# The second layer of a mixture of experts: two of three fp16 products of a term joined into one of 160 columns

## The chip, the cores and the metric

One core of a Trainium2 chip. The metric is the device time of one execution of the whole kernel in microseconds (us). TensorE is PE (PEld are its weight loads), VectorE is DVE, ScalarE is ACT, GpSimd is POOL, and SyncE (SP) starts the large transfers.

## What is computed

Attention over 8 batches, 8 heads, 576 positions and 64 columns a head (half of the heads with a local mask, half with a strided one); its result, 4608 tokens of 512 columns, goes through a mixture of 8 experts. Each token goes to the expert with the largest logit, and each expert takes at most 80 tokens, those with the largest gate weight:

```python
for e in range(E):
    ...
    h = np.maximum(x[tok_idx] @ w1[e], 0.0)          # 80x512 times 512x1024
    out[tok_idx] = gate_w[tok_idx, None] * (h @ w2[e])   # 80x1024 times 1024x512
```

The change is in the second product, `h @ w2[e]`.

## The kernel before

The first 235 us are attention, the gates and the choice of tokens. Then come the experts, the last 75 us, which the change touches.

Numbers are kept at fp32 accuracy by splitting: a weight is written as an upper part (fp16) and the rest (fp16), and so is an input. A product then has three terms: upper weights times upper input, upper weights times the rest, the rest of the weights times the upper input. `mm3` (lines 1148 to 1151) issues them as three matmuls of 80 columns (the 80 slots of an expert), each with its own load of 128x128 weights, all into the same place in PSUM. The term of the two rests is left out.

The weights come from HBM in 64 chunks of 512 KB (`wload`, L270), through eight staging tiles (`ring`, `raw`, `kst`). `wsplit` makes a chunk's two parts: ACT writes the upper part (L278), DVE the rest (L288). The next load of a staging tile is issued on SP's queue when DVE has read the tile. `spl` holds the parts of eight half layers.

The work goes by halves (`halves`): the first layer of an expert is `up`, the second `down_mm`. Their order is up(0), up(1), down(0), up(2), down(1), ..., up(7), down(6), down(7). In each half `weave` mixes the half's matmuls with two or three splits (by `BSPL`), and in an `up` half also with `xprep` (PE transposes the next expert's gathered tokens, ACT and DVE split them into `xe`, POOL starts a gather, L1092) and with `finish` (below) of the expert before. All engines execute their instructions in the order in which this emits them.

- `up` (L1153): for each of two groups, 4 x 4 x 3 matmuls into `hp`; ACT applies the ReLU and writes the upper part of `he` (L1164), DVE the rest (L1165). `he` is laid out part by part: first the eight blocks of the upper part, then those of the rest.
- `down_mm` (L1168): 4 x 8 x 3 = 96 matmuls into one tile `yp` of 320 columns, in two PSUM buffers; then ACT copies it to `y32` (L1185). For the last expert the eight blocks of the inner dimension are the outer loop, since its weights arrive last, and a product with zeros (L1172) opens the tile.
- `finish` (L1188): PE transposes `y32` (L1192), ACT multiplies by the gates (L1194), POOL scatters the rows to the output (L1195). It stands in the `up` half that follows the expert's `down_mm`, a little before the middle of it; for expert 6 in the last half, and for expert 7 at the end.

Of the kernel before, what the change touches and what calls it, by code (L numbers as in the profile page):

```python
# [9 lines left out]
F32 = mybir.dt.float32  # L10
BF16 = mybir.dt.bfloat16
F16 = mybir.dt.float16
I32 = mybir.dt.int32
U32 = mybir.dt.uint32
AF = mybir.ActivationFunctionType
ALU = mybir.AluOpType
AX = mybir.AxisListType
PSUM = bass.MemoryType.PSUM
DRAM = bass.MemoryType.DRAM

P = 128
B, H, S, D = 8, 8, 576, 64
DM = H * D
E, F = 8, 1024
# [6 lines left out]
SLOTS = 80  # L31
# [144 lines left out]
def moe_attention(ctx: ExitStack, tc, q, k, v, wg, w1, w2, cap, out):  # L176
    nc = tc.nc
# [10 lines left out]
    identb = const.tile([P, P], BF16, name="identb")  # L188
# [64 lines left out]
    def spl_of(h):  # L253
        return spls[h] if h < NPRE else (spls[NPRE:] + spls[:NPRE])[(h - NPRE) % len(spls)]
# [600 lines left out]
    for i in range(n + 2):  # L855
# [38 lines left out]
        if i in (18, 30):  # L894
            x = Bank()
# [4 lines left out]
        if i == n + 1:  # L900
            do_logits(B - 1)
            x = Bank()
# [171 lines left out]
    for j0 in range(0, NCAND, 8):  # L1074
        nc.vector.tensor_tensor(oh[:, j0:j0 + 8], iosl.unsqueeze(1).broadcast_to([P, 8, SLOTS]),
                                slot[:, j0:j0 + 8].unsqueeze(2).broadcast_to([P, 8, SLOTS]), op=ALU.is_equal)
        for j in range(j0, j0 + 8):
            nc.tensor.matmul(tab.rearrange("s e a -> s (e a)"), oh[:, j], val[:, j].rearrange("p e a -> p (e a)"),
                             start=(j == 0), stop=(j == NCAND - 1))
# [48 lines left out]
    ectx = ExitStack()  # L1128
    fp = ectx.enter_context(tc.tile_pool(name="fp", bufs=2))
    psx = ectx.enter_context(tc.tile_pool(name="psx", bufs=1, space=PSUM))  # L1130
    psh = ectx.enter_context(tc.tile_pool(name="psh", bufs=3, space=PSUM))
    psy = ectx.enter_context(tc.tile_pool(name="psy", bufs=2, space=PSUM))

    xes, hes, ys_ = {}, {}, {}
    zb = fp.tile([P, 4 * SLOTS], BF16, name="zb", bufs=1)
# [12 lines left out]
    def mm3(o, w, i, x, c, first, last):  # L1148
        nc.tensor.matmul(o, w[:, 0, i:i + P], x[:, 0, c], start=first, stop=False)  # L1149
        nc.tensor.matmul(o, w[:, 0, i:i + P], x[:, 1, c], start=False, stop=False)  # L1150
        nc.tensor.matmul(o, w[:, 1, i:i + P], x[:, 0, c], start=False, stop=last)  # L1151

    def up(h, e):  # L1153
        w, xe = spl_of(h), xes[e]
        he = hes[e] = fp.tile([P, 2, 8, SLOTS], F16, name="he")
        for f4 in range(2):
            hp = psh.tile([P, 4, SLOTS], F32, name="hp")
            for ff in range(4):
                for c in range(4):
                    mm3(hp[:, ff], w, F * c + P * (4 * f4 + ff), xe, c, c == 0, c == 3)  # L1160
                if ff < 3:
                    yield
            sl = slice(4 * f4, 4 * f4 + 4)
            nc.scalar.activation(he[:, 0, sl], hp, AF.Relu)  # L1164
            nc.vector.scalar_tensor_tensor(he[:, 1, sl], hp, 0.0, he[:, 0, sl], op0=ALU.max, op1=ALU.subtract)  # L1165
            yield

    def down_mm(h, e):  # L1168
        w, he = spl_of(h), hes[e]
        yp = psy.tile([P, 4, SLOTS], F32, name="yp")  # L1170
        if e == E - 1:
            nc.tensor.matmul(yp.rearrange("p f s -> p (f s)"), identb, zb, start=True, stop=False)  # L1172
        for c in range(8 if e == E - 1 else 0):
            for f in range(4):
                mm3(yp[:, f], w, DM * c + P * f, he, c, False, c == 7 and f == 3)
            yield
        for f in range(4 if e < E - 1 else 0):
            for c in range(8):
                mm3(yp[:, f], w, DM * c + P * f, he, c, c == 0, c == 7)
                if c == 3:  # L1180
                    yield
            if f < 3:
                yield
        y32 = ys_[e] = fp.tile([P, 4, SLOTS], F32, name="y32")
        nc.scalar.copy(y32, yp)  # L1185
        yield

    def finish(e):  # L1188
        y32 = ys_[e]
        yt = psy.tile([SLOTS, 4, P], F32, name="yt")  # L1190
        for f in range(4):
            nc.tensor.transpose(yt[:, f], y32[:, f], ident)  # L1192
        ys = fp.tile([SLOTS, DM], F32, name="ys")
        nc.scalar.activation(ys, yt.rearrange("s f p -> s (f p)"), AF.Copy, scale=gt[:, e:e + 1])  # L1194
        nc.gpsimd.indirect_dma_start(out=out, out_offset=bass.IndirectOffsetOnAxis(ap=ids[:, e:e + 1], axis=0),  # L1195
                                     in_=ys, in_offset=None, bounds_check=NT - 1, oob_is_err=False)
# [11 lines left out]
    for h, (e, w) in enumerate(halves):  # L1208
        tasks = [((down_mm if w else up)(h, e), 8, 0, 1)]
        m = BSPL[h % len(BSPL)]  # L1210
        tasks.append((splits(m), m, *WIN["b"]))
        if w == 0 and e + 1 < E:
            tasks.append((once(xprep, e + 1), 1, *WIN["bx"]))
        if w == 0 and e > 1:
            tasks.append((once(finish, e - 2), 1, *WIN["bf"]))
        if h == 2 * E - 1:
            tasks.append((once(finish, e - 1), 1, *WIN["bf"]))
        weave(*tasks)
        flush()
    finish(E - 1)  # L1220
    ms.close()
    ectx.close()
# [5 lines left out]
    with tc.If(flag > 0):  # L1228
        with tc.tile_pool(name="gp", bufs=1) as gp, tc.tile_pool(name="gw", bufs=1) as gw, \
# [18 lines left out]
            with tc.For_i(0, NT, P) as i:  # L1248
# [3 lines left out]
                x = gw.tile([P, DM], F32, name="gx")  # L1252
# [25 lines left out]
                for e in range(E):  # L1278
# [5 lines left out]
                    for f4 in range(2):  # L1284
                        hp = gps.tile([P, 4, P], F32, name="gt")
# [5 lines left out]
                    yp = gps.tile([P, DM], F32, name="gt")  # L1291
# [82 lines left out]
```

## Time and profile before

| | |
|---|---|
| time, median of 3 runs | 319.17 us (318.51 to 320.11) |
| profiled execution | 317.6 us, its span 315.9 us |
| PE busy | 265.2 us (84%), 5399 matmuls |
| DVE, ACT, POOL busy | 242.4, 225.3, 135.2 us |
| DMA | 84.27 MB, mean 267 GB/s |
| expert stage | from 235.95 us; last matmul of expert 7 at 308.21 us |

Times of the trace are counted from the start of the span. "Busy" of PE is a modelled figure, since matmuls overlap: a matmul's record lasts 0.20 us, while the next one starts 0.036 us later. A wait is put down to what released it; "issue" means that the engine waited for nothing that the profile shows.

### The profile page before, as it was taken

What the parts mean: (1) busy time and instruction counts of PE and PEld (TensorE: products, weight loads), DVE (VectorE), ACT (ScalarE), POOL (GpSimd) and SP (SyncE); (2) the same over time, 40 slices, a digit from 0 to 9 for tenths busy, and PEclk for the clock granted to TensorE, in tenths of its full rate; (3) what the DMA queues carried; (4) which work ended last, traced back from release to release, by engine and by line L of the source; (5) the groups of instructions that cost most, each with busy time, mean ns of one, the idle gap of its engine ahead of it and who ended that gap; (6) DMA issues with size and microseconds to landing.
All of it is one profiled execution on the core that took longest, in us unless ns stands there. A gap on an engine that the chain in (4) does not pass through costs nothing. (4 is left out here: it accounts for less than half of the span.)

```text
span 315.9 us, 12765 instructions
## 1 busy us (share of the span) xinstructions
PE 265.2 (84%) x5399; PEld 235.3 (74%) x5399; DVE 242.4 (77%) x487; ACT 225.3 (71%) x438; POOL 135.2 (43%) x156
## 2 busy tenths in 40 slices
PE   7997987998898899895979987967259969988891
PEld 7986876887767788875867866657249969988890
DVE  7497698989988699886678999361847987997860
ACT  1757777898798798795776876658107978987761
POOL 8658376267284367286265277013072221110012
PEclk9999999999999999998998999999776999999996
DMA  7999999899998799995789999689999999899501
GB/s 246 217 267 377 252 226 323 260 298 264 334 273 250 202 286 285 317 237 205 199 239 247 215 239 345 210 257 283 270 264 336 338 384 377 288 407 389 193 25 48
DMA packets 49375, 84.27 MB, mean 267 GB/s; under 512 B 23201, under 2 KB 23201, under 8 KB 49314
## 3 DMA queue, kind: packets, MB, share of 16 engines
q1 hardware_dynamic: 48290, 80.79, 86.4%
q0 software_dynamic: 1024, 2.62, 2.6%
q8 instruction: 44, 0.72, 1.0%
q14 instruction: 17, 0.14, 0.2%
HBM read 63.21 MB, written 20.19 MB: 264 GB/s over the span
## 5 line engine op out<-in xcount | busy, mean ns | idle before, releaser
L553 POOL TENSOR_TENSOR pb<-pb,sm 128x288 f32<-128x288 f32 (+2 forms) x32 | 34.9, 1092 | 61.1 <-DVE sm L551 44.3
L1150 PEld LDWEIGHTS <-spl 128*128 128x128 f16 x512 | 52.1, 102 | 3.7 <-issue 3.6
L1149 PEld LDWEIGHTS <-spl 128*128 128x128 f16 x512 | 52.1, 102 | 3.0 <-issue 3.0
L1151 PEld LDWEIGHTS <-spl 128*128 128x128 f16 x512 | 52.1, 102 | 2.1 <-issue 2.1
L461 POOL TENSOR_SCALAR vlo<-vlo 32x1152 f32<-32x1152 f32 (+1 forms) x32 | 37.7, 1179 | 6.8 <-DMA ring<-moe_w 2.2
L774 DVE SCALAR_TENSOR_TENSOR spl<-ring,spl 128x1024 f16<-128x1024 f32 x20 | 28.3, 1424 | 9.4 <-ACT spl L278 9.4
L1149 PE MATMUL hp<-xe,spl 128*128 128x80 f16 x256 | 31.7, 208 | 3.4 <-issue 2.8
L1150 PE MATMUL hp<-xe,spl 128*128 128x80 f16 x256 | 31.6, 207 | 1.4 <-issue 1.1
L1151 PE MATMUL hp<-xe,spl 128*128 128x80 f16 x256 | 31.6, 208 | 0.0
L598 PE MATMUL bank<-ptl,vlo 128*64 128x64 f32 x576 | 22.5, 228 | 9.4 <-issue 9.3
L353 ACT COPY ktl<-bank 64x384 f32<-64x384 f32 (+1 forms) x49 | 26.4, 566 | 4.8 <-DMA xs<-ktl 3.1
L1149 PE MATMUL yp<-he,spl 128*128 128x80 f16 x256 | 28.8, 202 | 1.2 <-issue 1.2
L1150 PE MATMUL yp<-he,spl 128*128 128x80 f16 x256 | 28.8, 202 | 1.1 <-issue 1.1
L1151 PE MATMUL yp<-he,spl 128*128 128x80 f16 x256 | 28.8, 202 | 0.4 <-issue 0.3
L1195 POOL DMA_INDIRECT out<-ys,ids x8 | 7.6, 950 | 50.1 <-ACT ys L1194 50.1
L598 PEld LDWEIGHTS bank<-ptl,vlo 128*64 128x64 f32 x576 | 19.5, 139 | 12.7 <-issue 10.6
L288 DVE SCALAR_TENSOR_TENSOR spl<-raw,spl 128x1024 f16<-128x1024 f32 x21 | 25.2, 1220 | 4.2 <-ACT spl L278 3.7
L278 ACT ACTIVATE spl<-ring 128x1024 f16<-128x1024 f32 x23 | 23.8, 1057 | 4.5 <-DMA ring<-moe_w 4.5
L353 ACT COPY ptl<-bank 64x256 f32<-64x256 f32 (+2 forms) x46 | 21.3, 473 | 6.8 <-PE bank L581 3.4
L549 DVE TENSOR_REDUCE sm<-pb 128x16 f32<-128x288 f32 (+2 forms) x32 | 22.8, 711 | 3.7 <-ACT pb L546 3.7
L546 ACT ACTIVATE pb<-pb 128x288 f32<-128x288 f32 (+2 forms) x32 | 18.1, 565 | 9.9 <-DVE pb L539 9.7
L353 ACT COPY xt<-bank 128x288 f32<-128x288 f32 (+3 forms) x40 | 16.8, 441 | 11.0 <-PE bank L598 7.7
(209 smaller groups left out, 752.7 us busy)
## 6 DMA issues: line engine op xcount, KB each, us to landing
ring<-moe_w SPq DMA_DIRECT2D x32, 512.0 KB
raw<-moe_w SPq DMA_DIRECT2D x21, 512.0 KB
raw<-q SPq DMA_DIRECT2D x16, 576.0 KB
out<-kst SPq DMA_DIRECT2D x9, 1024.0 KB
raw<-k SPq DMA_DIRECT2D x15, 576.0 KB
kst<-moe_w SPq DMA_DIRECT2D x11, 512.0 KB
xs<-xn SPq DMA_DIRECT2D x12, 384.0 KB
vs<-v SPq DMA_DIRECT2D x8, 512.0 KB
```

Of the source, the lines that this page charges most:

```text
L278: nc.scalar.activation(hi, r, AF.Copy, scale=SC)
L288: nc.vector.scalar_tensor_tensor(lo, r, SC, hi, op0=ALU.mult, op1=ALU.subtract)
L353: nc.scalar.copy(o, i)
L461: add(4 * b + m + 0.6 + 0.4 * u, "P", 1.25 if m == 0 else 1.1, lambda e: nc.gpsimd.tensor_scalar(vlo[64 * u:64 * u + 32, t0:t1], vlo[64 * ...
L546: add(pj(j) + E_EXP, "A", 0.13 + 0.83e-3 * nt * nk, lambda e: nc.scalar.activation(pa, pa, AF.Exp), wr=PN)
L549: nc.vector.tensor_reduce(each(sm[:, 0:nt], g), pq, op=ALU.add, axis=AX.X)
L553: add(pj(j) + E_MUL, "P", 0.2 + 1.7e-3 * nt * nk, lambda e: nc.gpsimd.tensor_tensor(plain(pa, g), plain(pa, g), spread(sm[:, 0:nt], g), op ...
L598: nc.tensor.matmul(o[64 * h:64 * h + 64, :, k0:k0 + 32], vlo[:, 2 * (t0 + c0 + c) + p, h], ptl[:, c0 + c, :, 32 * gg:32 * gg + 32], start= ...
L774: add(pr + 0.2, "V", 1.14, lambda e: nc.vector.scalar_tensor_tensor(lo, r, SC, hi, op0=ALU.mult, op1=ALU.subtract), rd=nm + [("hi", i)], l ...
L1149: nc.tensor.matmul(o, w[:, 0, i:i + P], x[:, 0, c], start=first, stop=False)
L1150: nc.tensor.matmul(o, w[:, 0, i:i + P], x[:, 1, c], start=False, stop=False)
L1151: nc.tensor.matmul(o, w[:, 1, i:i + P], x[:, 0, c], start=False, stop=last)
```

## The change

`mm2` takes the place of `mm3` in the second layer. One matmul multiplies the upper part of the weights by both parts of the input, 160 columns, into two neighbouring sums of 80 columns; a second one multiplies the rest of the weights by the upper part of the input and adds to the first of the two sums. For that `he` is laid out block by block, the two parts of a block side by side. The accumulator has twice the columns (640) and so takes two PSUM banks, `yp0` and `yp1`, one buffer each in place of two of one bank; `yt` keeps its two. ACT copies each bank to `y2`, the first when half of the half is done, and POOL adds the two sums into `y32`; for the last expert DVE adds. The zero product of the last expert becomes two. The first layer keeps `mm3`.

```diff
--- before.py
+++ after.py
@@ -1129,7 +1129,7 @@
     fp = ectx.enter_context(tc.tile_pool(name="fp", bufs=2))
     psx = ectx.enter_context(tc.tile_pool(name="psx", bufs=1, space=PSUM))
     psh = ectx.enter_context(tc.tile_pool(name="psh", bufs=3, space=PSUM))
-    psy = ectx.enter_context(tc.tile_pool(name="psy", bufs=2, space=PSUM))
+    psy = ectx.enter_context(tc.tile_pool(name="psy", bufs=1, space=PSUM))
 
     xes, hes, ys_ = {}, {}, {}
     zb = fp.tile([P, 4 * SLOTS], BF16, name="zb", bufs=1)
@@ -1152,7 +1152,8 @@
 
     def up(h, e):
         w, xe = spl_of(h), xes[e]
-        he = hes[e] = fp.tile([P, 2, 8, SLOTS], F16, name="he")
+
+        he = hes[e] = fp.tile([P, 8, 2, SLOTS], F16, name="he")
         for f4 in range(2):
             hp = psh.tile([P, 4, SLOTS], F32, name="hp")
             for ff in range(4):
@@ -1161,33 +1162,49 @@
                 if ff < 3:
                     yield
             sl = slice(4 * f4, 4 * f4 + 4)
-            nc.scalar.activation(he[:, 0, sl], hp, AF.Relu)
-            nc.vector.scalar_tensor_tensor(he[:, 1, sl], hp, 0.0, he[:, 0, sl], op0=ALU.max, op1=ALU.subtract)
+            nc.scalar.activation(he[:, sl, 0], hp, AF.Relu)
+            nc.vector.scalar_tensor_tensor(he[:, sl, 1], hp, 0.0, he[:, sl, 0], op0=ALU.max, op1=ALU.subtract)
             yield
+
+    def mm2(o, w, i, x, first, last):
+
+        nc.tensor.matmul(o.rearrange("p a s -> p (a s)"), w[:, 0, i:i + P], x.rearrange("p a s -> p (a s)"), start=first,
+                         stop=False)
+        nc.tensor.matmul(o[:, 0], w[:, 1, i:i + P], x[:, 0], start=False, stop=last)
 
     def down_mm(h, e):
         w, he = spl_of(h), hes[e]
-        yp = psy.tile([P, 4, SLOTS], F32, name="yp")
+        yp = [psy.tile([P, 2, 2, SLOTS], F32, name=f"yp{i}") for i in range(2)]
+        y32 = ys_[e] = fp.tile([P, 4, SLOTS], F32, name="y32")
+
+        def sums(i):
+            y2 = fp.tile([P, 2, 2, SLOTS], F32, name=f"y2{i}")
+            nc.scalar.copy(y2, yp[i])
+            (nc.vector if e == E - 1 else nc.gpsimd).tensor_tensor(y32[:, 2 * i:2 * i + 2], y2[:, :, 0], y2[:, :, 1], op=ALU.add)
         if e == E - 1:
-            nc.tensor.matmul(yp.rearrange("p f s -> p (f s)"), identb, zb, start=True, stop=False)
-        for c in range(8 if e == E - 1 else 0):
+            for t in yp:
+                nc.tensor.matmul(t.rearrange("p f a s -> p (f a s)"), identb, zb, start=True, stop=False)
+            for c in range(8):
+                for f in range(4):
+                    mm2(yp[f // 2][:, f % 2], w, DM * c + P * f, he[:, c], False, c == 7 and f % 2 == 1)
+                yield
+            for i in range(2):
+                sums(i)
+        else:
             for f in range(4):
-                mm3(yp[:, f], w, DM * c + P * f, he, c, False, c == 7 and f == 3)
-            yield
-        for f in range(4 if e < E - 1 else 0):
-            for c in range(8):
-                mm3(yp[:, f], w, DM * c + P * f, he, c, c == 0, c == 7)
-                if c == 3:
+                for c in range(8):
+                    mm2(yp[f // 2][:, f % 2], w, DM * c + P * f, he[:, c], c == 0, c == 7)
+                    if c == 3:
+                        yield
+                if f % 2:
+                    sums(f // 2)
+                if f < 3:
                     yield
-            if f < 3:
-                yield
-        y32 = ys_[e] = fp.tile([P, 4, SLOTS], F32, name="y32")
-        nc.scalar.copy(y32, yp)
         yield
 
     def finish(e):
         y32 = ys_[e]
-        yt = psy.tile([SLOTS, 4, P], F32, name="yt")
+        yt = psy.tile([SLOTS, 4, P], F32, name="yt", bufs=2)
         for f in range(4):
             nc.tensor.transpose(yt[:, f], y32[:, f], ident)
         ys = fp.tile([SLOTS, DM], F32, name="ys")
```

## Rows read from the trace of the kernel before

**Rows 1.** Windows: us, busy (count) of PE, PEld, DVE, ACT, POOL, PEclk, DMA share.
```profile
254.36:260.56 6.20, 5.06 (x128) 4.92 (x129) 4.73 (x7) 5.22 (x7) 1.04 (x2) 1.00 1.03 381
260.56:275.73 15.17, 14.82 (x383) 14.67 (x384) 13.28 (x16) 13.59 (x20) 2.09 (x2) 1.00 0.94 331
275.73:281.98 6.25, 5.19 (x128) 5.07 (x129) 5.53 (x8) 5.14 (x9) 0.86 (x1) 1.00 1.04 401
281.98:288.17 6.19, 4.74 (x128) 4.64 (x128) 6.19 (x7) 5.41 (x7) 0.05 (x1) 1.00 1.04 397
288.17:294.54 6.37, 5.21 (x129) 5.06 (x128) 4.25 (x5) 4.79 (x8) 0.91 (x1) 1.00 1.01 371
294.54:308.42 13.88, 13.88 (x363) 13.68 (x363) 9.43 (x11) 8.59 (x12) 1.59 (x2) 1.00 0.21 66
```

**Rows 2.** Waits of PE, 248 to 308.5 us (us in total, times, longest).
```profile
PE hp L1149 <- issue: 2.8, 2, 1.4
PE yp L1149 <- issue: 1.2, 1, 1.2
PE yp L1150 <- issue: 1.1, 1, 1.1
PE hp L1150 <- issue: 1.1, 1, 1.1
PE yp L1151 <- issue: 0.3, 1, 0.3
```

**Rows 3.** The page, DMA queues (packets, MB, share of 16 engines).
```profile
q8 instruction: 44, 0.72, 1.0%
```

**Rows 4.** DMA queues, 251.6 to 251.8, then 285.6 to 285.8 us.
```profile
q8 instruction: 1, 0.02, 40.5%
...
q8 instruction: 1, 0.02, 34.4%
```

**Rows 5.** Timeline of PE at restarts: start, duration, instruction, idle before.
```profile
254.36 0.21 PE L1149 MATMUL hp<-xe,spl 128*128 128x80 f16 x1 [1.36 <-issue]
...
288.17 0.20 PE L1149 MATMUL hp<-xe,spl 128*128 128x80 f16 x1 [1.45 <-issue]
```

**Rows 6.** Timeline of PE: a down half, transposes behind it, the last half.
```profile
265.90 0.20 PE L1149 MATMUL yp<-he,spl 128*128 128x80 f16 x1
...
269.34 0.20 PE L1149 MATMUL hp<-xe,spl 128*128 128x80 f16 x1
...
271.37 0.39 PE L1192 MATMUL yt<-ident,y 128*80 128x128 f32 x2
...
304.23 0.30 PE L1172 MATMUL yp<-zb,identb 128*128 128x320 bf16 x1
304.37 0.20 PE L1149 MATMUL yp<-he,spl 128*128 128x80 f16 x1
...
308.21 0.20 PE L1151 MATMUL yp<-he,spl 128*128 128x80 f16 x1
```

**Rows 7.** Timeline of ACT: copies of the sums, and a split.
```profile
270.02 0.41 ACT L1185 COPY y<-yp 128x320 f32<-128x320 f32 x1
...
284.38 1.05 ACT L278 ACTIVATE spl<-ring 128x1024 f16<-128x1024 f32 x1
...
304.49 0.43 ACT L1185 COPY y<-yp 128x320 f32<-128x320 f32 x1 [0.42 <-PE yp L1151]
```

**Rows 8.** Groups by line: adds on POOL and DVE (busy, mean ns; idle before).
```profile
L553 POOL TENSOR_TENSOR pb<-pb,sm 128x288 f32<-128x288 f32 x16 | 14.1, 885 | 24.0 <-DVE sm L551 18.2 <-DVE sg L696 5.0 <-ACT ptl L353 0.5
L1027 POOL TENSOR_TENSOR tok<-tok,tt 128x16 f32<-128x16 f32 x2 | 0.4, 221 | 0.2
...
L990 DVE TENSOR_TENSOR wgt<-cvi,segm 128x256 f32<-128x256 f32 x1 | 0.4, 424 | 0.0
```

**Rows 9.** Timeline of SP's queue: the first and last of twelve loads.
```profile
275.30 1.48 SPq L270 DMA_DIRECT2D ring<-moe_w  x2
...
293.54 0.37 SPq L270 DMA_DIRECT2D kst<-moe_w  x1
```

## The prediction

> **What bounds the kernel now.** I read first the windows over the expert stage, cut at the moments at which TensorE (PE) starts again after a gap [rows 1]. From 254.36 to 308.42 us PE is busy 48.90 of 54.06 us at the full granted clock (1.00), more than DVE (43.41), ACT (42.75) or POOL (6.54), and the DMA engines are full (share 1.01 to 1.04) nearly until 296. Then the waits of PE over the same time [rows 2]: five groups, 6.5 us in all, and each is "issue": no engine and no transfer releases PE. It waits neither for weights nor for an evacuation. So PE's own stream sets this stage, with its gaps, and after 294.5 PE has none.
>
> What the gaps are shows in the counts. Three times, between two gaps, PE executes 128 matmuls and 128 weight loads, 256 instructions, in 6.20, 6.25 and 6.37 us; in the long stretch 384 and 384, which is three times as many; 281.98 to 288.17 again 128 and 128 [rows 1] (single records are missing or lie on an edge). A transfer on the instruction queue, q8, of which the program has 44 [rows 3], comes some 2.5 us before each restart (I show two): one starts between 251.6 and 251.8 and PE restarts at 254.36, one between 285.6 and 285.8 and PE restarts at 288.17 [rows 4, 5]. 0.72 MB in 44 is 16 KB, 64 bytes for each of 256 instructions. I read from it that PE's instructions come in blocks of 256, that the next block is asked for when PE enters the present one, and that under full DMA queues it is there about 6.25 us later, while PE executes a block in about 4.9 us (15.17 us for three blocks less the last gap of 0.5). Each gap costs its idle time and the 0.17 us by which a record (0.20) outlasts the spacing of 0.036: 6.5 + 6 x 0.17 = 7.5 us between 248 and 295.
>
> [...]
>
> **The change part by part.** (a) Matmuls. A down half has 96 pairs of weight load and matmul, from 265.90 to 269.34, 35.8 ns each [rows 6]. Two of three become one of 160 columns: 64 pairs. The trace has no such matmul at 160; its neighbours are 80 columns (35.8 ns) and 320 columns (304.23 to 304.37, 140 ns) [rows 6]. Between them 160 costs 70.5 ns, so 106.3 for a pair of terms in place of 107.4: columns are streamed, and there are as many as before. Bounds: no gain, and 2 ns for each of 256; I take 0.3 us less in all. Taken alone that is nothing.
>
> (b) Instructions. Each of eight down halves issues 64 instructions fewer, 192 to 128; an expert's two halves with their transposes go from 400 to 336. The 400 last 400/256 x 4.9 = 7.7 us without gaps; the 336 take 7.6, so a block now holds 5.8 us of work. The wait at each block falls from 6.25 - 4.9 = 1.35 to 6.25 - 5.8 = 0.45 us. From 248 to 294.5 there are 46.5/6.25 = 7.4 such blocks; were every one late, 3.3 us would be lost; as before about one in four was not, I take 3.0. Saved: 7.5 - 3.0 = 4.5 us. Bounds: all 7.5 (every block in time), and nothing.
>
> (c) Evacuation. Two copies of 320 columns in place of one, 0.43 us each [rows 7], one behind the other. ACT is idle 11 us of the stage [rows 1], and eight more copies take 2.5: nothing for seven experts, as long as the queue behind them (splits, he, xe) has that room; a copy waits for PE, and the splits queued behind it wait too. POOL gets two adds an expert. Nearest rows: 221 ns at 16 columns, 885 at 288 [rows 8]; on the line between them 0.57 us at 160, bounds 0.22 and 0.89. POOL is idle for 47 of 54 us. Its sums are queued ahead of the scatter of the same expert, and behind that of an older one. [...] Who waits is PE: the four transposes of an expert come 2.03 us after its down half (269.34 to 271.37) [rows 6], and PE does everything behind them later. In that half the copy started at 270.02 and ended 0.94 us before the transposes [rows 7]. With 0.3 for the second copy (ACT starts the next operation 0.3 us after such a copy) and 0.57 for the sum 0.07 is left: nothing, but barely. he in its new layout has as many elements an operation: nothing.
>
> (d) One buffer. The first copy of a half is issued when half of it is done, so its bank is free early. The exception is the end: down(6) and down(7) follow each other, and the zero product into the second bank waits for the last copy of expert 6. That copy started at 304.49 and took 0.43 [rows 7], the first zero product is over at 304.37 [rows 6]: some 0.6 us of PE, on the path, and 0.14 for the second zero product (bounds 0.6, and 1.6 if a split of 1.05 us stands ahead of the copy).
>
> (e) The end. Between the last matmul (308.21) [rows 6] and the transposes stands one copy. Now a second follows, of which 0.2 us are won since the first bank is ready four pairs earlier: 0.1 more; then DVE's add. Rows: 424 ns at 256 columns [rows 8], for 160 I take 0.35 with the handover (bounds nothing and 0.42). Together 0.5 us; behind it the scatter and the end of the program are as before.
>
> Sum: -0.3 - 4.5 + 0.14 + 0.6 + 0.5 = -3.6 us. The profiled execution took 317.6 us (span 315.9); it would take 314.0. The median of the runs is 319.17, 1.6 above that execution; with the same difference 315.6 us.
>
> **The rivals.** 1. *The gaps stay as they are*: they are no late fetches, or the fetch gets as much slower as the blocks get longer. For it: the wait from request to arrival isn't constant (the three blocks after 260.56 came at 5.06 us each), so it depends on the traffic, and a faster PE makes the load queue fuller. Against: three times exactly 256 instructions. Then only -0.3 + 1.24 is left: 320.1 us. Chance 0.12.
>
> 2. *The loads become the bound.* The share is below 1.04 for 1.8 us in all until 294.5 (0.10 of 15.17, and little else) [rows 1]; loading can end only so much earlier. How far ahead of ACT the loads are I estimate by counting back: behind 294.54 the engines are busy for 0.21 x 13.88 = 2.9 us [rows 1], so the last load, issued at 293.54, is there by about 297.3; the one issued at 275.30 is the first of twelve [rows 9], eleven earlier, and at 512 KB by 400 GB/s (1.31 us each) there at 282.9; its split starts at 284.38 [rows 7]. So 1.5 us. PE can gain 1.8 + 1.5 = 3.3 us before ACT stands in front of an empty slot, with its copies queued behind: -3.3 - 0.3 + 1.24 = -2.4, 316.8 us. Chance 0.17.
>
> 3. *No gap at all*: if the fetch comes in 5.06 us as after 260.56, a block of 5.8 us hides it: -7.5 - 0.3 + 1.24 = -6.6, 312.6 us. Chance 0.10.
>
> 4. *Slower: PE waits for the sums.* Place: the transposes in each up half. Chain: ACT's queue, two copies, POOL's add, handovers. Price: it exceeds the 2.03 us as soon as two splits (2 us) stand ahead of the copy: 2.0 + 0.3 + 0.42 + 0.89 + 0.1 = 3.7, 1.7 us too late, or 2.0 with POOL slowed by DVE. An expert then takes 7.6 + 2.0 = 9.6 us, where before it took 9.1 (46.5 us for 2048 instructions, 400 an expert); over five experts +2.5, with the +0.94 of (a), (d) and (e) 322.6 us. It decides from a wait of 1.5 us in each half on. Against: in the half shown the copy stands behind one split and has 0.94 us to spare. Chance 0.08.
>
> **How the numbers follow.** My forecast has 0.53, at 315.6, itself uncertain by 2 (the number of late blocks). What a measurement of this kernel can tell from no change is about 0.5%, 1.6 us. Faster than 317.6: nearly all of the forecast, all of rival 3 and three quarters of rival 2: 0.75. Within: rival 1 for the most part, the rest of 2: 0.16. Slower: rival 4 and a little of 1: 0.09. The range goes from rival 3, 312.6, to 319.6, just short of rival 1.
>
> **What would show it.** Right: between gaps again 128 and 128 records, but over 5.8 us and more; "issue" of PE below 4 us where it was 6.5; two transfers fewer on q8; down halves as long as before (3.4 us); a PE wait of about 0.6 us at the second zero product; half a microsecond more between the last matmul and the last transposes. Wrong: "issue" as large as before with gaps at other counts (rival 1); ACT or DVE waiting for a DMA after 250 us (rival 2); PE waiting for POOL at the transposes (rival 4); down halves shorter than 3 us, which would mean that weight loads, not columns, were the limit.

## The result, and the profile after

The changed kernel takes 315.4 us (median of 4 runs, 313.73 to 315.96), the kernel before 319.64 us beside it (4 runs, 318.51 to 320.23): ratio 0.988, 95% interval 0.983 to 0.993. That is 4.2 us less; 3.6 less were forecast. The profiled execution after took 315.96 us, its span is 314.2 us.

The two profiled executions differ by 1.64 us only, since they also differ where their instructions are the same: the first expert's transposes begin at 235.95 us in before and at 239.94 in after, and over all profiles of this study between 235.95 and 243.82. The first two `up` halves, which are alike too, took 10.30 us in before and 9.40 in after, at a granted clock of 0.73 and 0.81. So the sharper measure of the change is the **expert part**, from the first matmul of down(0) to the last matmul of down(7). Within it the table adds up, from the matmul records, every distance from one start to the next of over 0.3 us ("gaps"); what is left is matmuls one behind the other. From here on *c1*, *c2* and *c3* are repeats of before and after.

| us | before | c1 (before) | after | c2 (after) | c3 (after) |
|---|---|---|---|---|---|
| expert part, from | 247.55 | 250.82 | 250.69 | 247.61 | 255.34 |
| to | 308.21 | 311.73 | 306.96 | 303.75 | 310.59 |
| its length | 60.66 | 60.91 | 56.28 | 56.14 | 55.24 |
| gaps in it | 7.75 | 8.27 | 4.28 | 3.94 | 2.80 |
| the rest | 52.91 | 52.64 | 52.00 | 52.20 | 52.44 |
| from the first transposes (the "stage" of some expectations) | 72.26 | 72.52 | 67.02 | 67.25 | 66.77 |
| end of the span behind it | 7.67 | 7.56 | 7.28 | 7.26 | 7.4 |

(The profiles of c3, and of e5 and e9 below, are of slow executions, whose attention part was long; what follows rests on their expert parts, where the granted clock was 1.00 in all three, and the ratios leave such executions out.) The expert part is 4.4 to 5.7 us shorter, and 3.5 to 5.5 us of that are gaps.

The windows of after, cut at PE's restarts, answer to [rows 1] (us, busy and count of PE, PEld, DVE, ACT, POOL, granted clock, DMA share, GB/s):

```profile
252.14:258.63 6.49, 6.14 (x128) 6.00 (x127) 6.49 (x7) 5.67 (x10) 3.67 (x3) 1.00 1.05 370
258.63:264.83 6.20, 5.83 (x128) 5.70 (x129) 6.20 (x8) 5.73 (x8) 2.43 (x4) 1.00 1.03 382
264.83:271.12 6.29, 6.12 (x128) 5.97 (x128) 5.71 (x8) 5.63 (x9) 1.38 (x2) 1.00 1.05 394
271.12:277.05 5.93, 5.67 (x129) 5.37 (x128) 5.93 (x7) 5.93 (x10) 2.59 (x3) 1.00 1.02 393
277.05:306.96 29.91, 29.29 (x618) 28.72 (x619) 27.79 (x29) 25.82 (x39) 10.35 (x12) 1.00 0.76 279
```

Between restarts there are again 128 matmuls and 128 loads, and the DMA engines are again full. What is new is that PE is busy for 5.67 to 6.14 us of such a stretch, where it was 4.74 to 5.21 in the stretches of before that end in a long gap. After 277.05 no crossing costs over 0.3 us; before, three after 281.9 cost 1.3 to 1.7 each. DVE is now busy in nearly all of it: from 250 to 300 us it waits for ACT's part of a split for 0.6 us, where it waited for 6.1 in before. The DMA engines stay full behind 277.05 too (share 1.03 until 296); the 0.76 of the last line is the mean with the end, where the loads are over.

A down half in after has 64 matmuls; its first one, and the first matmul behind it, where 3.44 us lay between the two in before ([rows 6]; PE's timeline):

```profile
259.79 0.23 PE L1171 MATMUL yp<-he,spl 128*128 128x160 f16 x1
...
263.15 0.20 PE L1149 MATMUL hp<-xe,spl 128*128 128x80 f16 x1
```

The waits of PE in after, 248 to 316 us, answer to [rows 2] (in total, times, longest):

```profile
PE yp L1171 <- DVE he L1166: 0.9, 1, 0.9
PE yt L1209 <- DVE y L1183: 0.8, 1, 0.8
PE yp L1173 <- issue: 0.4, 2, 0.3
PE yp L1186 <- ACT y L1182: 0.4, 1, 0.4
PE hp L1151 <- issue: 0.4, 1, 0.4
PE hp L1150 <- issue: 0.3, 1, 0.3
PE yt L1209 <- POOL y L1183: 0.2, 1, 0.2
```

"Issue" was 6.5 us and is 1.1. The 0.9 put down to DVE is no wait for DVE only: it ends at 252.14, which lies exactly one block of 256 instructions before 258.63 (first line of the windows); which of the two came last the profile doesn't tell. New are the 0.4 at the second zero product, 0.2 for POOL's sums, and 0.8 ahead of the last transposes, for DVE's add.

Two of the restarts in PE's timeline, with the idle time before them, answer to [rows 5], where it was 1.36 and 1.45:

```profile
258.63 0.21 PE L1150 MATMUL hp<-xe,spl 128*128 128x80 f16 x1 [0.35 <-issue]
...
277.05 0.21 PE L1173 MATMUL yp<-he,spl 128*128 128x80 f16 x1 [0.26 <-issue]
```

The instruction queue on the page after [rows 3]:

```profile
q8 instruction: 42, 0.69, 0.9%
```

The groups of after by line, 235 to 314 us (busy, mean ns; idle before), with the new operations and the splits:

```profile
L1171 PE MATMUL yp<-he,spl 128*128 128x160 f16 x256 | 28.4, 233 | 0.9 <-DVE he L1166 0.9
...
L288 DVE SCALAR_TENSOR_TENSOR spl<-raw,spl 128x1024 f16<-128x1024 f32 x21 | 26.6, 1288 | 1.0 <-ACT spl L278 1.0
...
L1183 POOL TENSOR_TENSOR y<-y 128x160 f32<-128x160 f32 x14 | 10.8, 773 | 23.8 <-ACT y L1182 23.8
...
L1182 ACT COPY y<-yp 128x320 f32<-128x320 f32 x16 | 6.6, 420 | 2.0 <-PE yp L1173 1.9
...
L1183 DVE TENSOR_TENSOR y<-y 128x160 f32<-128x160 f32 x2 | 0.6, 324 | 2.7 <-ACT y L1182 2.7
```

The same splits (those out of `raw`) in before (groups by line, 232 to 311 us) took 1220 ns:

```profile
L288 DVE SCALAR_TENSOR_TENSOR spl<-raw,spl 128x1024 f16<-128x1024 f32 x21 | 25.2, 1220 | 4.2 <-ACT spl L278 3.7 <-issue 0.5
```

The end of after in the timelines of PE, ACT and DVE (start, duration, instruction, idle before) answers to [rows 6, 7]:

```profile
302.34 0.30 PE L1186 MATMUL yp<-zb,identb 128*128 128x320 bf16 x1
303.07 0.30 PE L1186 MATMUL yp<-zb,identb 128*128 128x320 bf16 x1 [0.43 <-ACT y L1182]
...
306.96 0.20 PE L1173 MATMUL yp<-he,spl 128*128 128x80 f16 x1
307.95 0.67 PE L1209 MATMUL yt<-ident,y 128*80 128x128 f32 x4 [0.79 <-DVE y L1183]
...
302.59 0.43 ACT L1182 COPY y<-yp 128x320 f32<-128x320 f32 x1
...
307.05 0.75 ACT L1182 COPY y<-yp 128x320 f32<-128x320 f32 x2 [0.79 <-PE yp L1173]
...
307.57 0.58 DVE L1183 TENSOR_TENSOR y<-y 128x160 f32<-128x160 f32 x2 [2.74 <-ACT y L1182]
```

and the same place in before:

```profile
309.61 0.63 PE L1192 MATMUL yt<-ident,y 128*80 128x128 f32 x4 [1.19 <-ACT y L1185]
...
309.13 0.42 ACT L1185 COPY y<-yp 128x320 f32<-128x320 f32 x1 [1.66 <-PE yp L1151]
```

The last transposes come 0.99 us after the last matmul (307.95 - 306.96) where they came after 1.40 (309.61 - 308.21), in spite of a second copy and an add.

### The profile page after: what moved, and what is told of

Same layout as the page of the kernel before. It is cut to its first block, busy times and chain, and to the rows that moved or that the text cites. A ratio compares the mean times of both kernels' runs of the same rounds, so it can differ in the third digit from the quotient of the medians.

```text
span 314.2 us, 12290 instructions
## 1 busy us (share of the span) xinstructions
PE 268.0 (85%) x5144; PEld 235.9 (75%) x5144; DVE 244.9 (78%) x489; ACT 227.7 (72%) x446; POOL 147.4 (47%) x170
## 3 DMA queue, kind: packets, MB, share of 16 engines
q1 hardware_dynamic: 48290, 80.79, 87.4%
## 5 line engine op out<-in xcount | busy, mean ns | idle before, releaser
L598 PE MATMUL bank<-ptl,vlo 128*64 128x64 f32 x576 | 24.0, 236 | 9.3 <-issue 8.8
L1149 PE MATMUL hp<-xe,spl 128*128 128x80 f16 x256 | 30.8, 205 | 0.6 <-ACT xe L1143 0.6
L1150 PE MATMUL hp<-xe,spl 128*128 128x80 f16 x256 | 30.7, 205 | 0.7 <-issue 0.3
L1151 PE MATMUL hp<-xe,spl 128*128 128x80 f16 x256 | 30.7, 205 | 0.4 <-issue 0.4
L598 PEld LDWEIGHTS bank<-ptl,vlo 128*64 128x64 f32 x576 | 20.8, 147 | 12.7 <-issue 10.8
L1171 PE MATMUL yp<-he,spl 128*128 128x160 f16 x256 | 28.4, 233 | 0.9 <-DVE he L1166 0.9
L1173 PE MATMUL yp<-he,spl 128*128 128x80 f16 x256 | 28.0, 199 | 0.4 <-issue 0.4
L288 DVE SCALAR_TENSOR_TENSOR spl<-raw,spl 128x1024 f16<-128x1024 f32 x21 | 26.6, 1288 | 1.0 <-ACT spl L278 1.0
L1150 PEld LDWEIGHTS <-spl 128*128 128x128 f16 x256 | 26.1, 102 | 1.3 <-issue 1.2
L1151 PEld LDWEIGHTS <-spl 128*128 128x128 f16 x256 | 26.1, 102 | 0.9 <-issue 0.9
L1149 PEld LDWEIGHTS <-spl 128*128 128x128 f16 x256 | 26.2, 102 | 0.0
L1173 PEld LDWEIGHTS <-spl 128*128 128x128 f16 x256 | 25.0, 98 | 1.4 <-issue 1.4
L1171 PEld LDWEIGHTS <-spl 128*128 128x128 f16 x256 | 25.1, 98 | 0.9 <-issue 0.9
L628 ACT ACTIVATE pts<-bank,hm 72x288 f32<-72x288 f32 x52 | 21.9, 494 | 3.8 <-DVE pts L622 2.0
```

The source lines that it names most:

```text
L288: nc.vector.scalar_tensor_tensor(lo, r, SC, hi, op0=ALU.mult, op1=ALU.subtract)
L598: nc.tensor.matmul(o[64 * h:64 * h + 64, :, k0:k0 + 32], vlo[:, 2 * (t0 + c0 + c) + p, h], ptl[:, c0 + c, :, 32 * gg:32 * gg + 32], start= ...
L1171: nc.tensor.matmul(o.rearrange("p a s -> p (a s)"), w[:, 0, i:i + P], x.rearrange("p a s -> p (a s)"), start=first, stop=False)
L1173: nc.tensor.matmul(o[:, 0], w[:, 1, i:i + P], x[:, 0], start=False, stop=last)
```

## The experiments

The theory: PE stands still where the next block of 256 instructions, which comes through the same DMA engines as the weights (the page after gives the loads' queue, q1, and q8 as shares of the same 16 engines, 87.4% and 0.9%), isn't there yet, and the change gains because it does the same columns with fewer instructions. The main rival: the gain comes from something else in the change (the evacuation in halves, the second bank, fewer weight loads), and the count of instructions is incidental.

| | time, us (runs) | ratio to before, 95% | expert part | gaps | rest | stage |
|---|---|---|---|---|---|---|
| e1_split | 319.29 (10) | 1.003 [0.998, 1.009] | 60.62 | 6.85 | 53.77 | 71.23 |
| e2_loads | 321.49 (4) | none | 62.40 | 2.59 | 59.81 | 73.24 |
| e4_before_half | 310.47 (4) | 0.977 [0.958, 0.997] | 52.88 | 0 | 52.88 | 63.88 |
| e5_after_half | 316.52 (10) | 0.982 [0.969, 0.995] | 53.95 | 1.78 | 52.17 | 65.84 |
| e6_nosum | 315.89 (10) | 0.995 [0.988, 1.002] | 55.37 | 2.55 | 52.82 | 66.15 |
| e3_hybrid | 315.65 (12) | 0.991 [0.986, 0.996] | 56.71 | 4.56 | 52.15 | 67.31 |
| e7_late | 316.53 (12) | 0.991 [0.984, 0.997] | 54.84 | 2.71 | 52.13 | 66.77 |
| e8_late_again | 316.35 (12) | 0.996 [0.990, 1.002] | 54.38 | 2.29 | 52.09 | 65.41 |
| e9_finish_late | 316.04 (12) | 0.989 [0.984, 0.994] | 55.86 | 3.86 | 52.00 | 66.53 |

**c1_before and c2_after** are the two kernels once more, as they are, for a second profile of each (columns c1 and c2 of the first table).

> The kernel before once more, for a second profile of it. Theory: gaps at blocks of 256 instructions, 5 to 7 of them over 0.4 us; stage from the first expert transposes to the last matmul 71.5 to 73 us (first profile 72.3). If the first profile was an odd one, less than 70.

> The changed kernel once more, for a second profile of it: stage 66 to 68 us (first profile 67.0); up to 2 us more where POOL's second sum of the first expert takes 3.5 us, as in two of the four profiles so far that have these sums.

Measured: expert parts of 60.91 and 56.14 us, within 0.3 of the first profiles, though the transposes before them begin up to 3.4 us earlier or later. The gain in the expert part is no accident of one execution.

**e1_split** takes the join back and leaves everything else of the change (two banks, copies in halves, sums on POOL):

```diff
-        nc.tensor.matmul(o.rearrange("p a s -> p (a s)"), w[:, 0, i:i + P], x.rearrange("p a s -> p (a s)"), start=first,
-                         stop=False)
+        if first:
+            nc.tensor.matmul(o.rearrange("p a s -> p (a s)"), w[:, 0, i:i + P], x.rearrange("p a s -> p (a s)"),
+                             start=True, stop=False)
+        else:
+            nc.tensor.matmul(o[:, 0], w[:, 0, i:i + P], x[:, 0], start=False, stop=False)
+            nc.tensor.matmul(o[:, 1], w[:, 0, i:i + P], x[:, 1], start=False, stop=False)
```

> The changed kernel with the join alone undone: every product of 160 columns but the first of each sum (and none of them in the last expert) is two of 80 columns again, with a weight load each; the two banks, the copies, POOL's sums and the layout of he stay. A down half issues 184 instructions in place of 128 (192 in the kernel before). Theory (PE's instructions come in blocks of 256, and a block that is used up before the next is there stops PE): the gaps of 1.1 to 1.6 us return, 5 or 6 of them, the stage from the first expert transposes to the last matmul is again 72 to 73.5 us (before 72.3, after 67.0), and the time 319 to 321 us, at or above the kernel before, as the evacuation costs what it cost. Rival (the gain is from the two banks and the earlier copy): stage 67, time 315 to 316 us.

Measured: the time of before (319.29 beside 320.01) and its expert part (60.62). The windows between two restarts late in it, the waits of PE (246 to 315 us), and a window behind its longest wait:

```profile
284.42:290.34 5.92, 4.88 (x129) 4.78 (x128) 5.92 (x8) 5.92 (x9) 3.35 (x3) 1.00 1.01 381
290.34:296.63 6.29, 5.30 (x128) 5.16 (x127) 6.01 (x8) 5.43 (x10) 1.28 (x3) 1.00 1.04 385
...
258.00:261.25 3.25, 3.21 (x50) 3.13 (x51) 1.27 (x3) 2.52 (x3) 1.93 (x2) 0.58 1.02 390
```

```profile
PE yt L1213 <- POOL y L1187: 1.6, 1, 1.6
PE hp L1151 <- issue: 1.2, 2, 1.0
...
PE yp L1177 <- issue: 1.0, 1, 1.0
PE hp L1150 <- issue: 0.8, 1, 0.8
```

A block takes PE 4.9 to 5.3 us again, and "issue" rises from 1.1 to 3.0 us. By the times of ten executions the rest of the change gains nothing without the join. The profile, whose stage of 71.23 us is below the 72 to 73.5 expected, isn't as clean as the times: gaps at block crossings are 3.8 us here (1.02, 0.38, 1.24, 1.19), less than the 7.75 of before. Another part is one wait of 1.6 us for a POOL sum. Behind it no block is late until 284.42, but the granted clock is 0.58 on the mean from 258.00 to 261.25, and until 260.7 the matmuls start 67 ns apart in place of 36. Less that wait and some 1.1 us for the lower clock (an estimate, see the last section) the expert part would be 57.9 us, between before and after. So it is the times that say that the join is what gains; how much of it is fetched blocks, this run doesn't say.

**e2_loads** leaves the joined matmuls and adds two weight loads that nothing needs to each pair of terms, so that a down half has 192 instructions as before, at 64 matmuls in place of 96:

```diff
         nc.tensor.matmul(o.rearrange("p a s -> p (a s)"), w[:, 0, i:i + P], x.rearrange("p a s -> p (a s)"), start=first,
                          stop=False)
+        for _ in range(2):
+            nc.tensor.ldweights(w[:, 0, i:i + P])
```

> The changed kernel with two more weight loads behind each product of 160 columns, which nothing uses: the matmuls are those of the changed kernel, the instructions of a down half are 192 again as before. Theory (the count of instructions decides): the gaps return at every 256 instructions, with fewer matmuls between them than 128; stage 71.5 to 73.5 us, time 319 to 321 us. Rival (the number of matmuls or the shape decides, instructions don't): no gap of over 0.6 us, stage 67 to 68, time 315 to 316 us. If the loads themselves don't hide behind the 67 ns of a product, the down halves last longer than 3.4 us without gaps; that would be a third outcome, to be told apart by their length between gaps.

Measured: an expert part of 62.40 us, longer than before, but not by gaps. A down half takes 4.26 us in place of 3.36: 64 more loads, 0.90 / 64 = 14 ns each. The loads aren't hidden, so a block holds more work and is late less often: this is the third outcome of the expectation, and the experiment can't price a late block. It does settle what is counted. Its window between two restarts:

```profile
259.39:265.57 6.18, 5.41 (x116) 5.30 (x139) 4.72 (x6) 5.07 (x8) 2.58 (x3) 1.00 1.04 377
```

**e4_before_half and e5_after_half** halve the traffic and nothing on PE: of each weight chunk that is loaded in the expert stage only half is fetched, in the kernel before and in the changed one.

```diff
+        if i >= NCH * NPRE + NST:
+            if w == 0:
+                dst, src = dst[:, 0:CH // 2], src[:, 0:CH // 2]
+            else:
+                dst, src = dst[:, 0], src[:, 0]
         nc.sync.dma_start(dst, src)
```

> The kernel before, but from the 29th chunk on each weight load moves only its first half (the rest of the staging tile keeps old values, so the output is not the reference's): in the expert stage half the traffic, the same instructions and the same waits. Theory (a block of PE's instructions is late because its transfer stands behind the weight loads): the gaps of 1.1 to 1.6 us vanish or shrink below 0.5, although nothing on PE has changed; stage 64.5 to 66.5 us (before 72.3), time 312 to 314 us. Rival (the gaps are PE's own, a cost of the crossing whatever the traffic): the gaps stay, stage 71 to 73.

> The changed kernel with the same half traffic (same limits on the output). Theory: with the blocks in time there is nothing for the change to win, and what it adds shows alone: as fast as the kernel before with half traffic or slower, by 0 to 1.2 us, stage 65 to 67. Rival (the change wins by its matmuls or its evacuation): still 4 us faster than the other.

Measured: in e4 PE, with the instructions of before, never stops. The window of its whole middle, and the waits of PE in e5 from 247 us on:

```profile
252.44:294.45 42.01, 42.01 (x1105) 41.94 (x1102) 41.46 (x47) 40.15 (x58) 11.33 (x7) 1.00 0.68 205
```

```profile
PE yt L1214 <- DVE y L1188: 0.8, 1, 0.8
PE yt L1214 <- POOL y L1188: 0.5, 2, 0.3
PE yp L1191 <- ACT y L1187: 0.4, 1, 0.4
```

The first and the last matmul of the expert part, in e4 and then in e5 (PE's timeline):

```profile
249.00 0.20 PE L1154 MATMUL yp<-he,spl 128*128 128x80 f16 x1
...
301.88 0.20 PE L1156 MATMUL yp<-he,spl 128*128 128x80 f16 x1
```

```profile
253.69 0.23 PE L1176 MATMUL yp<-he,spl 128*128 128x160 f16 x1
...
307.64 0.20 PE L1178 MATMUL yp<-he,spl 128*128 128x80 f16 x1
```

This is the pair that decides. With the DMA engines at 0.68 in place of 1.01 to 1.04 [rows 1], all six gaps of before are gone, though nothing was waiting for a weight [rows 2]; the expert part falls by 7.8 us to 52.88, which is what was left of before without its gaps (52.91). And with blocks in time the change *costs*, in this one pair of profiles: e5's expert part is 53.95, 1.07 us longer than e4's. (By the stage they are 1.96 apart, more than the 1.2 that were expected at most, as the part ahead was longer in e5.) In e5 the last two halves take 7.99 us in place of 7.42, PE waits twice for POOL, and the six other down halves are 0.08 us shorter each. So the change gains only where blocks come late; the joined matmul itself is worth 0.6 us and the evacuation takes more than that. The times of the two (310.47, and 316.52 with 308.78 to 318.74) point the same way but scatter too much to price it: in the profiles alone e5's expert part begins 4.7 us later, at 253.69 and 249.00.

The traces also show which part of a fetch the traffic makes longer. I take each block of PE for one transfer of 16 KB on q8: the page has 44 of them and 10798 matmuls and weight loads in before, 42.2 times 256, and 42 and 10288, 40.2 times 256, in after. One in before, when the loads are over, and one in e4 (DMA queues, 300.3 to 300.5 and 284.4 to 284.6 us):

```profile
q8 instruction: 1, 0.02, 28.0%
...
q8 instruction: 1, 0.02, 30.7%
```

Such a share of 16 engines in 0.2 us makes the transfers 0.90 and 0.98 us long; by [rows 4] two under the full queues took 1.30 and 1.10. Over the whole expert part they take 0.88 to 1.30 us in before and 0.88 to 1.73 in e4. So the transfer itself is no shorter with half the traffic. What differs is when it starts. Ahead of a gap of before it starts 3.3 to 3.9 us after PE enters the block before it (281.98 in [rows 1], and 285.6 to 285.8 in [rows 4]), and PE restarts 1.3 to 1.4 us after its end. In e4, with the crossings counted at the same matmuls, it starts 0.2 to 2.0 us after PE enters the block; in before, with the loads over, 0.8 us (299.50 by count) and less. The full queues delay the start of the transfer, not the transfer.

**e6_nosum** leaves POOL's and DVE's sums out (it transposes the first of the two sums alone, so the output lacks the second term):

```diff
-        y32 = ys_[e] = fp.tile([P, 4, SLOTS], F32, name="y32")
+        y32 = ys_[e] = []
...
-            (nc.vector if e == E - 1 else nc.gpsimd).tensor_tensor(y32[:, 2 * i:2 * i + 2], y2[:, :, 0], y2[:, :, 1], op=ALU.add)
+            y32.append(y2)
...
-            nc.tensor.transpose(yt[:, f], y32[:, f], ident)
+            nc.tensor.transpose(yt[:, f], y32[f // 2][:, f % 2, 0], ident)
```

> The changed kernel without the additions of the two sums: the transposes read the first sum straight from ACT's copy, so the product of the upper weights with the rest of the input is missing from the output. Theory: POOL's sums are hidden for seven experts, so only the last addition (0.3) and the one wait of PE on POOL seen (0.2) go: 0.4 to 0.8 us less than the changed kernel; DVE's splits are back from 1295 to 1220 ns. Rival (the sums hold PE or DVE in every expert): 2 us less or more.

Measured: the stage is 66.15 us, 0.9 less than in the first profile of after; but by the expert part it has 55.37 against 56.28, 56.14 and 55.24, no more than repeats of after differ. The time shows no gain either. The splits are at their old length (groups by line, 235 to 313 us):

```profile
L288 DVE SCALAR_TENSOR_TENSOR spl<-raw,spl 128x1024 f16<-128x1024 f32 x21 | 25.2, 1219 | 1.2 <-ACT spl L278 0.6 <-issue 0.5
```

So the sums are what makes the splits 1288 ns long, and no effect of it on PE is seen beyond what repeats differ by.

**e3_hybrid** keeps the change for seven experts and does the last one as before (three matmuls a term, one bank, one zero product, one copy, no add):

```diff
-        yp = [psy.tile([P, 2, 2, SLOTS], F32, name=f"yp{i}") for i in range(2)]
+        yp = [psy.tile([P, 2, 2, SLOTS], F32, name=f"yp{i}") for i in range(1 if e == E - 1 else 2)]
...
-            for t in yp:
-                nc.tensor.matmul(t.rearrange("p f a s -> p (f a s)"), identb, zb, start=True, stop=False)
+            y = yp[0].rearrange("p f a s -> p (f a) s")
+            nc.tensor.matmul(y.rearrange("p f s -> p (f s)"), identb, zb, start=True, stop=False)
...
-                    mm2(yp[f // 2][:, f % 2], w, DM * c + P * f, he[:, c], False, c == 7 and f % 2 == 1)
+                    mm3(y[:, f], w, DM * c + P * f, he.rearrange("p c a s -> p a c s"), c, False, c == 7 and f == 3)
...
-            for i in range(2):
-                sums(i)
+            nc.scalar.copy(y32, y)
```

> The changed kernel, but the last expert's second layer as before: three products of 80 columns, one bank, one zero product, one copy, no sum. Theory: the wait at the second zero product (0.43 and 0.14 us), the second copy (0.33) and the sum (about 0.3) leave the path, and since the loads are over by then the instruction blocks come early enough for the 64 instructions more: 1.0 to 1.3 us less than the changed kernel, 314.2 to 314.5 us, stage 66.4. Rival (the late block returns in the last half): a gap of about 1 us in the last two halves, and no gain over the changed kernel.

Measured: the last two halves take 7.34 us in place of 7.99, as the zero product's wait is gone. But 315.65 is no other time than that of after, and its profile has a wait of 2.4 us for one POOL sum (timeline of POOL, then the waits of PE from 249 us on):

```profile
255.78 3.52 POOL L1183 TENSOR_TENSOR y<-y 128x160 f32<-128x160 f32 x1 [1.41 <-ACT y L1182]
```

```profile
PE yt L1208 <- POOL y L1183: 2.8, 3, 2.4
```

**e7_late, e8_late_again, e9_finish_late and c3_after** try to win that wait back. e7 is e3 with the transposes of an expert late in the `up` half; e8 is e7 again; e9 is after with the late transposes alone; c3 is after, beside e8 and e9.

```diff
-            tasks.append((once(finish, e - 2), 1, *WIN["bf"]))
+            tasks.append((once(finish, e - 2), 1, *WIN["bl"]))
...
-WIN = dict(b=(0.2, 1), bx=(0.12, 0.55), bf=(0.45, 0.56))
+WIN = dict(b=(0.2, 1), bx=(0.12, 0.55), bf=(0.45, 0.56), bl=(0.8, 0.95))
```

> The changed kernel with the last expert's second layer as before (three products of 80 columns, one bank, one copy) and with the transposes of an expert's sums late in the up half (at 0.88 of it in place of 0.5), so that POOL has some 3.4 us for its sums in place of 2.0. Theory: PE no longer waits for POOL (0.2 us in the changed kernel's profile, 1.6 and 2.4 us in two others), and the end is shorter by one copy, one sum and the zero product's wait: stage 65.5 to 66.5 us in every profile, time 313.5 to 314.5 us. Rival (these waits were cover for late blocks, which return in their place): stage 67, time 315 to 316 us.

> The changed kernel once more, as the measure for the two kernels beside it. The expert part is now counted from the first matmul of the first down half to the last matmul of the second layer, since the first two up halves, whose instructions are the same in all kernels, run at a granted clock that differs from profile to profile (0.73 in the profile of before, 0.81 in the one of after). By that count the two profiles of after so far have 56.3 and 56.1 us, and those of before 60.7 and 60.9. Theory: 56.2 again, within 0.4 us, and a time of 313 to 316.5 us.

> The kernel with the transposes of an expert late in the up half and the last half with three matmuls a term, once more. By the count from the first down half its profile had 54.8 us, 1.4 less than after. Theory 1 (a true gain, of the zero product's wait, of the longer last half and of the waits for POOL): 54.3 to 55.3 us again, and a time some 1.3 us below that of after in the same set. Theory 2 (the blocks of instructions happened to come earlier in that one profile): 55.6 to 56.4, and no difference in the times.

> The changed kernel with one edit: the transposes of an expert stand late in the following up half (from 0.8 of it on, in place of 0.45), the last half as in after. Theory 1: no wait of PE for POOL's sums is left, and the wait of 0.43 us at the second zero product stays; 55.4 to 56.0 us from the first down half, 0.2 to 0.8 less than after, of which the times can show nothing. Theory 2 (late transposes move the block crossings so that more of them come late): 56.2 or more.

Measured: e7's stage of 66.77 is longer than was expected, in part since its first two `up` halves took 10.59 us; its expert part, 54.84, has no wait for POOL of 0.2 us or more, but a late block came back in the last half but one (0.87 us, at 299.29). e8 has 54.38, as theory 1 says; c3 has 55.24, 1 us below the 56.2 that were expected of it and outside the 0.4 that were allowed: so far can the expert part of one kernel differ from profile to profile. So e7's form is 0.4 to 1.9 us shorter in the expert part than the profiles of after, and the times don't show it: 316.35 beside 317.58 us by the medians, while the ratios (0.996, and 0.992 with 0.986 to 0.998) stand the other way round, with intervals that overlap. e9 has 55.86, in the range of theory 1, but not for its reason: PE still waits for POOL, since a sum took 3.51 us here too.

```profile
PE yt L1209 <- POOL y L1183: 0.6, 1, 0.6
```

None of these is shown to be faster than the changed kernel.

## Why the prediction was right, and where its steps were off

**The bound and the gaps.** Right. Between restarts lie 256 instructions in before and after, and e2 shows that it is instructions and not matmuls (116 + 139 = 255, a record lies on an edge). e4 shows the cause: less traffic, no gap. That speaks against rival 1: the crossings cost 7.75 us of 60.66 in before and nothing in e4. That the next block is asked for when PE enters the present one was read from two transfers; the traces show no request, but none of the transfers in before or e4 starts ahead of that moment as counted. That it is there about 6.25 us later is no fixed time: most of it is the 3.3 to 3.9 us until the transfer starts. And the blocks behind 260.56, which the prediction takes for fetches of 5.06 us (rivals 1 and 3), show how long PE worked in them, not when the next block came; in them the transfer starts 2.1 to 3.3 us after PE enters.

**(a) Matmuls,** -0.3. Half the size: a down half without gaps takes 3.36 us in after and 3.44 in before, 0.08 less, -0.6 if all eight are alike (the last two can't be read singly).

**(b) Instructions,** -4.5. Right in mechanism, and 0.2 to 1 us too small. The term was 7.5 us of gaps falling to 3.0. Measured at block crossings (in the expert part, without the waits for POOL, for ACT and at the zero product): 7.75 and 8.27 before; 3.09 in after (1.07, 0.55, 0.57, 0.40, 0.50), 2.4 in c2 and 2.1 in c3. So -4.7 in the first pair and -5.5 on the mean. The step said that blocks still come 6.25 us apart and PE waits for 0.45 us at each: they came 5.93 to 6.49 apart, with 0.17 to 0.37 us of idle time where the profile names issue alone. That one block in four isn't late was too careful: after 277 hardly any was. The share of the DMA engines doesn't explain that: it is 1.03 until 296 there too, and yet the transfers start 1.7 to 3.1 us after PE enters a block (by count) in place of 3.3 to 3.9. What lets them start earlier is open.

**(c) Evacuation,** nothing, "but barely". The estimate of the POOL add, 0.57 us, was too low: 0.77 on the mean, 0.53 to 1.51 in after. The bound of 0.89 didn't hold, and four profiles have a sum of 3.3 to 3.7 us. PE waits for POOL for 0.2 us in after, 0.5 in c2, 0.5 in e5, and 2.8 at worst (e3). So rival 4's mechanism is there, but in one to three halves rather than in each; the long waits (e1, e3) come from a slow sum, not from splits ahead of the copy. POOL slowed by DVE, which rival 4 prices at 0.3 us, is in the timelines of after: the four sums that begin beside an L1166 of DVE took 0.53 us each, the ten that begin within one of its splits 0.57 to 1.51, and each of the ten ends 0.45 to 0.48 us after DVE's next operation begins. DVE loses too: a split takes 1288 ns on the mean in place of 1220, and DVE is busy 49.42 of the 50 us from 250 to 300. No cost of it is seen (e6), but of the 10.7 us that DVE was idle in before (54.06 less 43.41, [rows 1]) next to nothing is left.

**(d) One buffer,** +0.6 and +0.14. Right: the second zero product starts 0.73 us after the first, and the matmuls 0.13 behind it.

**(e) The end,** +0.5. The sign was wrong: -0.4. The copies and the add cost what was said (0.75 and 0.58 us, 0.23 of it side by side), but the copy begins 0.09 us after the last matmul's start (some 0.3 after the last one of its own bank, which is four pairs earlier), where in before it began 0.92 after it (309.13 and 308.21). The step took that delay for a fixed part of the end. In before the copy behind the last half but one began 0.26 after the zero product that follows that half (304.49 and 304.23) [rows 6, 7], so the row to doubt the delay by was there. What makes the 0.92 is open: e3 and e7, whose end has the form of before, have a wait of PE of 1.2 us there again, but e8, the same kernel as e7, has 0.6.

**The sum.** By the steps the expert part and the end were to lose 3.6 us. The expert part lost 4.4 in the first pair, 4.9 by the means (60.8 and 55.9), and the end 0.3 to 0.4. The time lost 4.2 in the first set of runs and 3.3 in the last (320.92 and 317.58; ratio 0.992, 0.986 to 0.998). So the traces lost 1.2 to 1.6 us more than was forecast, of which (e) is 0.9; the rest is, in the main, (a) and (b) less the waits for POOL, and doesn't add up to better than some tenths. The times lost about what was forecast; their interval, 2.3 to 5.4 us in the first set, holds both. That 315.6 lies 0.2 from the median is therefore partly luck.

**The rivals.** Rival 2 (the loads become the bound) didn't occur: from 250 to 300 us neither PE nor ACT nor DVE waits for a load, though the DMA share was 1.02 to 1.05 until 296. Rival 3 (no gap) is what the later half of the stage came near to.

## What to carry to other kernels

Where PE's waits are "issue", count instructions between two restarts: if the number is the same each time (here 256), suspect that the limit is how many instructions a piece of work takes, and take traffic away to test it (e4). Here joining matmuls then paid, though the columns stayed the same: with the DMA engines full (a share of 1.01 to 1.05) the expert part was 4.4 to 5.7 us shorter. Price such a change as (time to the next block) minus (work in a block), and ask what it is worth with blocks in time; here, with a DMA share of 0.68 and 0.69, that was a loss of 1.07 us by one pair of profiles, hidden under a gain of five. Where executions differ before the changed part begins, compare lengths between two instructions that enclose it.

## What the hardware showed beside that

A sum of POOL that takes 0.5 to 1.6 us otherwise (2.2 once each in e8 and e9) takes 3.3 to 3.7 us in e1, e3, e8 and e9, always the second one of the first expert. It isn't the sum: in e6, which has none, the gather near that time is as long (and in e4, of the form of before, 3.05 us at 254.47).

```profile
255.74 3.18 POOL L1092 DMA_INDIRECT xg<-xs,idx  x1 [6.31 <-PE xp L1141]
```

In the profile of before that gather took 1.17 us, at 253.28. The cause is open, and so is whether POOL was busy in that time. The change lets PE depend on it, which it didn't before.

In e1 the granted clock fell in the wait of 1.62 us (1.00 from 256.15 to 257.30, 0.51 from there to 258.04), and behind it the matmuls started 67 ns apart for 2.2 us, at a granted clock of 0.50. It cost some 1.1 us beside the wait itself (an estimate: 33 matmuls at 67 ns in place of 36, and the transposes ahead of them, two of which last 0.65 us where two before the wait lasted 0.39). PE had stood still for 1.02 us shortly before, until 255.74. In e3, where PE had worked from 251.60 to 256.68 without such a gap, the clock stayed at 1.00 through a wait of 2.41 us and behind it (to 261.40). What decides that isn't shown.

A weight load that no matmul needs wasn't free beside the others: in e2 each cost 14 ns, where a matmul of 80 columns with its own load takes 35.8 [rows 6].
